# Attention over a long cache on one core: V of B in one megabyte transfer a step, issued by ScalarE instead of SyncE

## The chip, the cores and the metric

One core of a Trainium2 chip runs the whole program. The metric is device time in microseconds (us), as the median of several executions. Before: 859.62 us, median of 3 runs (857.61 to 861.04). With one core there is no second die to compare with.

## The reference, cut to what matters

Two attention blocks stand side by side, and their outputs are concatenated. A has 32 query heads on 4 K/V heads; B has 32 query heads on 32 K/V heads. B therefore reads eight times as much cache as A.

```python
B, Sq, D = 16, 32, 1024
Hq, Hkv, Sk, Dh = 32, 4, 1024, 128     # A;  B: H = 32 heads of K and V
q = (x @ wq) ...                        # per head
scores = einsum("bhqd,bhkd->bhqk", q, k) * Dh ** -0.5
p = softmax(scores)
o = einsum("bhqk,bhkd->bhqd", p, v)
out = o ... @ wo                        # bf16; A and B concatenated
```

K and V of B are 134 MB each, out of 338 MB that are read.

## The kernel before: the parts that matter

The kernel records operations with the buffers that they read and write. A list scheduler then puts them in order with a model of their durations, and each engine gets its own stream of instructions in that order. Semaphore waits are inserted. Each engine works through its own stream in order, and the streams meet only at semaphores.

There are 128 steps for B. A step needs 1 MB of K and 1 MB of V (four heads of one batch element); A's K and V, wq and wo come in between. K has two buffers and V has three. K goes through a DVE transpose, PE makes the scores, ScalarE the exponentials, PE transposes P, and then PE makes the product with V (L947, "the product" below). The product frees V's buffer.

```python
def st_dmaV(q):                                   # V of B; all loads are issued by "sp", SyncE
    ...
    sl = q.vslot                                  # t % 3
    for t_ in range(2):                           # two transfers of 512 KB
        vsrc = pb["v"][q.b, q.h0 + 2 * t_:q.h0 + 2 * t_ + 2].rearrange("a (p c) d -> p a c d", c=NCH)
        pr.add("sp", lambda e, ...: e.dma_start(VB_sb[:, sl, 2 * t_:2 * t_ + 2, :, :], vsrc),
               writes=[("VB", sl, t_)], dma_key=f"vb{sl}_{t_}", name="vb_dma", dur=2 * Sk * Dh * 2, ...)
```

The scheduler's model has one line for the DMA. It holds SyncE's loads back, so that none is issued more than 1.5 us before the modelled DMA is free. This hold applies to `"sp"` alone.

```python
if op.eng == "sp":
    st = max(st, dma_free[0] - SP_AHEAD)          # 1.5 us; SyncE's loads only
...
if op.dma_key is not None:
    free[op.eng] = st + 0.06                      # cost of an issue on its engine
    xs = max(st + 0.06, dma_free[0])              # first in, first out
    dma_free[0] = xs + op.dur / dma_bw
    op.t1 = dma_free[0] + dma_lat
...
seq = sorted(range(n), key=lambda k: (ops[order[k]].t0, k))   # the order of all streams
```

On the chip nothing holds SyncE back except the semaphores. The model gives the order alone.

## Time and profile before

| | before |
|---|---|
| time, median | 859.62 us |
| busy: PE, DVE, ACT | 84%, 63%, 52% |
| DMA, 40 to 835 us | 407 GB/s |
| DMA idle, worked out from the trace's packets | 15.6 us, of which 12.3 in the last 25 us and 1.2 in the middle |
| V of B: mean time from landing to its product | 1.9 us |

"DMA idle" is the busy time of the packets in each microsecond, summed over the 16 DMA engines and divided by 16, taken from one. I worked it out from the packet records. "Middle" is from 40 us to 25 us before the end.

These are lines of the page of before: busy time of the engines, busy tenths and GB/s in 40 slices, the one DMA queue, the chain that ended last by engine, two groups (line, engine, operation, tiles, count, then busy us and mean ns of one, then idle time just before them with what ended most of it), and DMA issues (KB each, median us to landing).

```profile
PE 717.3 (84%) x11970; PEld 436.2 (51%) x12098; DVE 541.5 (63%) x1115; ACT 447.1 (52%) x981; POOL 67.9 (8%) x76
...
DMA  9999999999999999999999999999999999999994
GB/s 341 366 400 412 413 412 389 413 415 399 413 400 385 413 410 412 402 400 411 403 412 404 406 411 401 411 408 408 413 403 412 412 409 412 414 411 409 411 384 174
...
q1 hardware_dynamic: 135424, 339.78, 101.1%
...
DMA 53%; PE 19%; DVE 15%; SPq 6%; issue 4%; ACT 2%; POOL 1%; POOLq 0%; DVEq 0%
...
L820 DVE STREAM_TRANSPOSE KBt_sb<-KB_sb 128x1024 f32<-128x1024 f32 x256 | 306.1, 1226 | 97.7 <-DMA KB_sb<-in_B_k_cache_dram 93.9
...
L947 PE MATMUL ps_o<-VB_sb,PT_sb 128*32 128x128 bf16 x4096 | 81.6, 221 | 23.7 <-DMA VB_sb<-in_B_v_cache_dram 16.6
...
KB_sb<-in_B_k_cache_dram SPq DMA_DIRECT2D x128, 1024.0 KB, 9.1
VB_sb<-in_B_v_cache_dram SPq DMA_DIRECT2D x256, 512.0 KB, 9.8
...
wq_sb<-in_A_wq_dram SPq DMA_DIRECT2D x32, 256.0 KB, 8.5
woB_sb<-in_B_wo_dram SPq DMA_DIRECT2D x32, 256.0 KB, 10.8
```

The DMA row of the slices is full to the last slice. The row of GB/s and the queue at 101.1% say the same: the DMA is the bound.

Windows of before (stretch; length; busy time of PE, PEld, DVE, ACT, POOL; granted clock; DMA share; GB/s), and the first projection in its timeline:

```profile
40.00:835.00 795.00, 679.54 (x11507) 415.32 (x11618) 515.91 (x1067) 430.40 (x948) 65.56 (x63) 0.97 1.03 407
```

```profile
17.01 3.47 PE L668 MATMUL ps_pj<-xT_sb,wq_sb 128*128 128x512 bf16 x8 [0.88 <-DVE xT_sb L584]
```

### The profile page before, as it was taken

What the parts mean: (1) busy time and instruction counts of PE and PEld (TensorE: products, weight loads), DVE (VectorE), ACT (ScalarE), POOL (GpSimd) and SP (SyncE); (2) the same over time, 40 slices, a digit from 0 to 9 for tenths busy, and PEclk for the clock granted to TensorE, in tenths of its full rate; (3) what the DMA queues carried; (4) which work ended last, traced back from release to release, by engine and by line L of the source; (5) the groups of instructions that cost most, each with busy time, mean ns of one, the idle gap of its engine ahead of it and who ended that gap; (6) DMA issues with size and microseconds to landing.
All of it is one profiled execution on the core that took longest, in us unless ns stands there. A gap on an engine that the chain in (4) does not pass through costs nothing.

```text
span 857.6 us, 27298 instructions
## 1 busy us (share of the span) xinstructions
PE 717.3 (84%) x11970; PEld 436.2 (51%) x12098; DVE 541.5 (63%) x1115; ACT 447.1 (52%) x981; POOL 67.9 (8%) x76
## 2 busy tenths in 40 slices
PE   3999998898978789888897979988889778878885
PEld 2546655455545455555554545545455445545452
DVE  1655566666657477577674756757777656666674
ACT  1456766466544464546554545544565554555452
POOL 0001000100000000000000000000000000000000
PEclk9999999999999999999999989999999999999898
DMA  9999999999999999999999999999999999999994
GB/s 341 366 400 412 413 412 389 413 415 399 413 400 385 413 410 412 402 400 411 403 412 404 406 411 401 411 408 408 413 403 412 412 409 412 414 411 409 411 384 174
DMA packets 135547, 341.57 MB, mean 398 GB/s; under 512 B 10496, under 2 KB 26880, under 8 KB 119040
## 3 DMA queue, kind: packets, MB, share of 16 engines
q1 hardware_dynamic: 135424, 339.78, 101.1%
q8 instruction: 96, 1.57, 0.7%
q14 instruction: 27, 0.22, 0.1%
HBM read 337.64 MB, written 2.10 MB: 396 GB/s over the span
## 4 chain that ended last, share of the span: by engine, by line
DMA 53%; PE 19%; DVE 15%; SPq 6%; issue 4%; ACT 2%; POOL 1%; POOLq 0%; DVEq 0%
DMA KB_sb<-in_B_k_cache_dram 40%; DVE KBt_sb L820 12%; DMA VA_sb<-in_A_v_cache_dram 5%; PE ps_pj L709 4%; PE ps_s L855 3%; DMA woA_sb<-in_A_wo_dram 3%; PE ps_pj L651 3%; PE ps_pj L668 2%; SPq L800 2%; PE ps_o L947 2%; PE ps_kt L913 2%; SPq L682 1%; PE ps_s L838 1%; PE ps_pt L897 1%; DMA woB_sb<-in_B_wo_dram 1%
## 5 line engine op out<-in xcount | busy, mean ns | idle before, releaser
L820 DVE STREAM_TRANSPOSE KBt_sb<-KB_sb 128x1024 f32<-128x1024 f32 x256 | 306.1, 1226 | 97.7 <-DMA KB_sb<-in_B_k_cache_dram 93.9
L878 ACT ACTIVATE P_sb<-ps_s 128x512 bf16<-128x512 f32 x256 | 152.4, 600 | 84.1 <-PE ps_s L855 74.5
L870 ACT ACTIVATE PTA_sb<-ps_s 128x1024 bf16<-128x1024 f32 x128 | 131.3, 1026 | 104.2 <-PE ps_s L838 91.5
L855 PE MATMUL ps_s<-KBt_sb,QB_sb 32*32 32x512 bf16 x4096 | 146.9, 395 | 10.1 <-DVE KBt_sb L820 5.5
L582 ACT COPY PT_sb<-ps_pt 128x512 f32<-128x512 f32 x128 | 74.9, 585 | 105.7 <-PE ps_o L947 88.6
L794 POOL COPY VAp_sb<-VA_sb 128x1024 bf16<-128x1024 bf16 x64 | 66.6, 1041 | 761.9 <-DMA VA_sb<-in_A_v_cache_dram 729.4
L897 PE MATMUL ps_pt<-id,P_sb 128*128 128x128 f32 x512 | 105.5, 305 | 9.3 <-ACT P_sb L878 7.3
L947 PE MATMUL ps_o<-VB_sb,PT_sb 128*32 128x128 bf16 x4096 | 81.6, 221 | 23.7 <-DMA VB_sb<-in_B_v_cache_dram 16.6
L897 PEld LDWEIGHTS ps_pt<-id,P_sb 128*128 128x128 f32 x512 | 82.7, 206 | 35.2 <-ACT P_sb L878 17.7
L947 PEld LDWEIGHTS ps_o<-VB_sb,PT_sb 128*32 128x32 bf16 x4096 | 60.0, 97 | 60.2 <-issue 56.9
L913 PE MATMUL ps_kt<-VAp_sb,PTA_sb 128*128 128x129 bf16 x1024 | 80.8, 222 | 10.9 <-POOL VAp_sb L794 4.9
L913 PEld LDWEIGHTS ps_kt<-VAp_sb,PTA_sb 128*128 128x128 bf16 x1024 | 67.5, 99 | 36.5 <-POOL VAp_sb L794 14.9
L838 PE MATMUL ps_s<-QT_sb,KTA_sb 128*128 128x256 bf16 x512 | 82.2, 275 | 3.0 <-DVE KTA_sb L584 2.0
L855 PEld LDWEIGHTS ps_s<-KBt_sb,QB_sb 32*32 32x32 bf16 x4096 | 49.3, 90 | 60.9 <-DVE KBt_sb L820 10.6
L709 PE MATMUL ps_pj<-woA_sb,OTA_sb 128*128 128x512 bf16 x224 | 64.0, 394 | 17.4 <-DMA woA_sb<-in_A_wo_dram 10.0
L963 DVE TENSOR_SCALAR OB_sb<-ps_o,rinv_all 128x128 bf16<-128x128 f32 x128 | 43.7, 342 | 53.4 <-PE ps_o L947 52.6
L709 PE MATMUL ps_pj<-woB_sb,OTB_sb 128*128 128x512 bf16 x206 | 62.0, 394 | 16.6 <-ACT OTB_sb L582 4.5
L668 PE MATMUL ps_pj<-xT_sb,wq_sb 128*128 128x512 bf16 x234 | 64.2, 389 | 8.4 <-DMA wq_sb<-in_B_wq_dram 3.4
L651 PE MATMUL ps_pj<-xT_sb,wq_sb 128*128 128x512 bf16 x232 | 63.9, 380 | 8.3 <-DMA wq_sb<-in_A_wq_dram 4.1
L883 DVE TENSOR_TENSOR stat<-stat 64x1 f32<-64x1 f32 x256 | 41.9, 164 | 32.0 <-ACT P_sb L878 24.4
L838 PEld LDWEIGHTS ps_s<-QT_sb,KTA_sb 128*128 128x128 bf16 x512 | 45.0, 98 | 25.5 <-issue 4.4
L722 DVE TENSOR_TENSOR acc<-acc,ps_pj 128x512 f32<-128x512 f32 x64 | 43.0, 672 | 20.1 <-PE ps_pj L709 19.7
(49 smaller groups left out, 533.0 us busy)
## 6 DMA issues: line engine op xcount, KB each, us to landing
KB_sb<-in_B_k_cache_dram SPq DMA_DIRECT2D x128, 1024.0 KB, 9.1
VB_sb<-in_B_v_cache_dram SPq DMA_DIRECT2D x256, 512.0 KB, 9.8
KA_sb<-in_A_k_cache_dram SPq DMA_DIRECT2D x64, 256.0 KB, 10.3
VA_sb<-in_A_v_cache_dram SPq DMA_DIRECT2D x64, 256.0 KB, 9.6
wq_sb<-in_B_wq_dram SPq DMA_DIRECT2D x32, 256.0 KB, 8.6
wq_sb<-in_A_wq_dram SPq DMA_DIRECT2D x32, 256.0 KB, 8.5
woB_sb<-in_B_wo_dram SPq DMA_DIRECT2D x32, 256.0 KB, 10.8
woA_sb<-in_A_wo_dram SPq DMA_DIRECT2D x32, 256.0 KB, 10.1
```

The source lines that it names most:

```text
L582: pr.add("act", lambda e: e.copy(dst_ap, src_ap), reads=reads, writes=writes, name=name + "@act", wtag=wtag, rtag=rtag)
L651: last = e.matmul(ps_pj[:, 0:tn], wq_sb[:, 0, j, hc * Dh:(hc + 1) * Dh], xT_sb[:, 0, j, t0:t0 + tn], start=(j == 0), stop=(j == DJ - 1))
L668: last = e.matmul(ps_pj[:, 0:NTOK], w, xT_sb[:, 1, j, :], start=(j == 0), stop=(j == DJ - 1))
L709: last = e.matmul(ps_pj[:, 0:OUTW], OT[:, gp, hh, :], wo_[:, hh, oh * OUTW:(oh + 1) * OUTW], start=(hh == 0), stop=(hh == nh - 1))
L820: pr.add("dve", lambda e: e.transpose(KBt_sb[:, sl, t_, :].bitcast(F32).rearrange("p (s r i) -> p s r i", r=2, i=32), KB_sb[:, rs, t_, :]. ...
L838: last = e.matmul(ps_s[:, sbf, c2, i * 2 * P:(i + 1) * 2 * P], KTA_sb[:, sl, c * P:(c + 1) * P], qt, start=True, stop=True)
L855: last = e.matmul(ps_s[32 * cg:32 * cg + 32, sbf, g, :].rearrange("p (sh cl j) -> p sh cl j", sh=4, cl=4), lhsT, kt[32 * a:32 * a + 32, g, ...
L870: pr.add("act", lambda e: e.activation(dst, src, ACTF.Exp, scale=scale), writes=BK_S[sbf] + [("PTA", q.half)], name="expA", rtag={("Sv", s ...
L878: pr.add("act", lambda e, src=src, dst=dst, g=g: e.activation(dst, src, ACTF.Exp, scale=scale, accum_out=st[:, g:g + 1]), writes=[BK_S[sbf ...
L897: last = e.transpose(ps_pt32[:, m * P:(m + 1) * P], p32[:, m:Sk // 2:NPK], id32[:])
L913: last = e.matmul(ps_kt[:, qh * OA0:qh * OA0 + Dh + 1], PTA_sb[:, h, c, qh * P:(qh + 1) * P], VAp_sb[:, sl, 4 * h + c, 0:Dh + 1], start=(h ...
L947: last = e.matmul(ps_o[32 * a:32 * a + 32, 0:Dh], PT_pairs[:, c // 2, 32 * (a ^ (c // 4 * 2)):32 * (a ^ (c // 4 * 2)) + 32, c % 2], VB_sb[ ...
```

## The change

The intent is to take 256 issues from SyncE and to let V be requested as soon as its buffer is free, by ScalarE, in transfers twice as large. (In the page of after, ScalarE's loads show as a DMA queue of their own, q10.) The scheduler also gets a more honest cost for an issue.

```diff
+DMA_ISSUE = 0.45
...
-                free[op.eng] = st + 0.06
-                xs = max(st + 0.06, dma_free[0])
+                free[op.eng] = st + DMA_ISSUE
+                xs = max(st + DMA_ISSUE, dma_free[0])
...
-                for t_ in range(2):
-                    vsrc = pb["v"][q.b, q.h0 + 2 * t_:q.h0 + 2 * t_ + 2].rearrange("a (p c) d -> p a c d", c=NCH)
-                    pr.add("sp", lambda e, t_=t_, vsrc=vsrc: e.dma_start(VB_sb[:, sl, 2 * t_:2 * t_ + 2, :, :], vsrc), writes=[("VB", sl, t_)],
-                           dma_key=f"vb{sl}_{t_}", name="vb_dma", dur=2 * Sk * Dh * 2, wtag={("VB", sl, t_): q.kid})
+                vsrc = pb["v"][q.b, q.h0:q.h0 + 4].rearrange("a (p c) d -> p a c d", c=NCH)
+                pr.add("act", lambda e: e.dma_start(VB_sb[:, sl, :, :, :], vsrc), writes=[("VB", sl)],
+                       dma_key=f"vb{sl}", name="vb_dma", dur=4 * Sk * Dh * 2, wtag={("VB", sl): q.kid})
...                                        (the product's reads follow: ("VB", kvs) in place of two halves)
```

V is now an `"act"` operation, so the scheduler no longer holds it back.

More of the change, by code (lines that the diff above doesn't have):

```diff
@@ L211, in odur @@
             if op.dma_key is not None:
-                return 0.06 + op.dur / dma_bw + dma_lat
+                return DMA_ISSUE + op.dur / dma_bw + dma_lat
             return op.dur
@@ L950, in st_pv @@
             for c0 in range(0, NCH, 2):
-                pr.add("pe", lambda e, c0=c0: e_pv(e, c0), reads=["PT", ("VB", kvs, 0), ("VB", kvs, 1)], writes=[BK_O], name="PVB",
-                       dur=0.116, tag="B%d" % q.t, rtag={"PT": q.qid, ("VB", kvs, 0): q.kid, ("VB", kvs, 1): q.kid}, wtag={"Ops": q.qid})
+                pr.add("pe", lambda e, c0=c0: e_pv(e, c0), reads=["PT", ("VB", kvs)], writes=[BK_O], name="PVB",
+                       dur=0.116, tag="B%d" % q.t, rtag={"PT": q.qid, ("VB", kvs): q.kid}, wtag={"Ops": q.qid})
         def st_recip(q):
```

## The prediction

> **What bounds the kernel now.** The DMA. In the slices of the page the 16 DMA engines are busy nine tenths or more in 39 of 40, and the queue table puts 101.1% of their span on one queue. Between 40 and 835 us they move 407 GB/s; the transposes of K (the costliest DVE group) wait 93.9 us for K to land, and the chain that ended last is 53% DMA, 40% of it loads of K of B. PE is busy 84%, DVE 63%, ACT 52%. From 20 us to the last steps at least 12 packets are in flight at nearly every moment. A fit of packet counts per 3 us stretch gives 80 ns of a DMA engine for a 2 KB packet (92160 of them, V among them), 313 ns for 8 KB (16384, K) and 44 ns for 1 KB (16384): together, with semaphore writes, about 839 us of 16 engines. The rest of 858 is the start (2 to 3 us) and a tail of some 15 us, where the last slice falls to 174 GB/s.
>
> **What the change does.** It removes no byte and leaves V's packets at 2 KB; only 128 transfers fewer complete: 2048 semaphore packets of 9 to 10 ns, 1.3 us over 16 engines. SyncE loses 256 issues (170 us of its sequencer in the trace, 0.47 us median, up to 3.2 us when some 1400 descriptors are outstanding). ScalarE gains 128 issues, each of 512 descriptors; my estimate from SyncE's 0.34 us (128 descriptors) and 0.47 us (256) is 0.5 to 0.9 us, so 65 to 115 us: ScalarE's occupancy rises from 52% to 60 to 65%. With 2% of the chain, this costs almost nothing. SyncE's waits no longer hold V back, but they never emptied the DMA engines, so there is little to gain. The Trainium skill ("DMA: Bandwidth & Descriptors", section "Issuing engines are not separate DMA queues") says that both issuers share the same 16 DMA engines and that a second one saves only sequencer time; this trace, with one issuer, cannot show it.
>
> **Where it can cost.** At the start the three V buffers are free, so ScalarE issues 3 MB of V at once, which competes with x, wq and the first K. The projections start at 17.0 us now; I expect 20 to 23 us. As V is then already loaded, the DMA engines have less to do while compute starts: 1 to 5 us lost. In the steady state V is always ahead and K shares bandwidth with it; buffers fill instead, and the DMA engines stay busy: zero change. In the tail the last K rather than the last V lands late: 0 to 3 us more.
>
> **Sum.** 859.6 - 1.3 + 3 (start) + 0 (steady) + 1 (tail) = about 862 us; range 850 to 877. Faster by over 2%: 0.07; within 2%: 0.80; slower: 0.13.
>
> **What would show each step.** A second DMA queue with about 134 MB; 40 to 835 us still at 400 to 415 GB/s; V issues on ScalarE's queue of 0.5 to 0.9 us and no waits there of many microseconds; first projection later than 17.0 us; K of B still the main DMA of the chain; PE's waits for V gone.
>
> **What would make it wrong.** If ScalarE blocks in a V issue (backpressure, or a wait for the product that frees V's buffer), the exponentials are late and PE, at 84%, becomes the bound: slower by 2 to 5%. If two rings let a DMA engine overlap packets better than one, the 80 ns per 2 KB packet falls and the kernel gains 1 to 3%. If K gets too small a share beside V, its transposes, scores and all buffers stall together: slower.

## More of the kernel before

Waits of before (engine, line, releaser: us in total, times, longest us):

```profile
DVE KBt_sb L820 <- DMA KB_sb<-in_B_k_cache_dram: 93.9, 82, 3.1
...
PE ps_o L947 <- DMA VB_sb<-in_B_v_cache_dram: 16.6, 27, 1.6
```

DVE waits often for K, but never long. PE waits little for V. Waits of PE and of its weight loads overlap, so I quote matmuls only.

All loads stand in SyncE's queue, and each needs about 9 us from issue to landing although 1 MB alone takes about 2.6 us at 407 GB/s. That is a backlog, and it keeps the DMA fed.

## The result, and the profile after

The changed kernel took 902.78 us (median of 4 runs, 896.74 to 909.97). Before, in the same rounds: 859.26 us (857.61 to 861.04). The ratio is 1.0509, with a 95% interval of 1.0425 to 1.0594: slower by 5%. Ratios here are the mean time of one kernel's fast runs over that of the other's of the same rounds, so not quite the ratio of the medians that are quoted.

The same lines of the page of after:

```profile
PE 731.2 (81%) x11975; PEld 442.2 (49%) x12098; DVE 539.2 (60%) x1115; ACT 447.0 (49%) x981; POOL 67.9 (8%) x76
...
DMA  9998999989999999999999999999899999999892
GB/s 347 411 360 296 369 409 405 410 321 415 379 402 414 414 357 392 390 412 406 405 402 406 411 392 400 410 406 356 303 408 363 401 369 414 411 403 409 284 383 83
...
q1 hardware_dynamic: 65792, 205.55, 57.6%
q10 hardware_dynamic: 67584, 134.23, 39.5%
...
DMA 46%; PE 31%; DVE 14%; ACT 3%; issue 2%; SPq 2%; POOL 1%; ACTq 0%; DVEq 0%; POOLq 0%
...
L820 DVE STREAM_TRANSPOSE KBt_sb<-KB_sb 128x1024 f32<-128x1024 f32 x256 | 306.1, 1224 | 60.6 <-DMA KB_sb<-in_B_k_cache_dram 52.0
...
L947 PE MATMUL ps_o<-VB_sb,PT_sb 128*32 128x128 bf16 x4096 | 84.8, 227 | 49.0 <-DMA VB_sb<-in_B_v_cache_dram 40.7
...
VB_sb<-in_B_v_cache_dram ACTq DMA_DIRECT2D x128, 1024.0 KB, 11.6
KB_sb<-in_B_k_cache_dram SPq DMA_DIRECT2D x128, 1024.0 KB, 8.2
...
wq_sb<-in_A_wq_dram SPq DMA_DIRECT2D x32, 256.0 KB, 10.9
woB_sb<-in_B_wo_dram SPq DMA_DIRECT2D x32, 256.0 KB, 12.6
```

Total bytes are the same, and there are two queues, 205.55 and 134.23 MB, as predicted. But the DMA row has gaps and the GB/s row has holes (296, 321, 303, 284). PE stands idle 49.0 us before the product with V, instead of 23.7, most of it for V's transfer. ScalarE's own busy time is unchanged.

```profile
DVE KBt_sb L820 <- DMA KB_sb<-in_B_k_cache_dram: 52.0, 45, 3.8
...
PE ps_o L947 <- DMA VB_sb<-in_B_v_cache_dram: 40.7, 21, 4.4
```

DVE waits less for K than before, and PE's matmuls wait 40.7 us for V instead of 16.6. So V, which was to be early, is late before 21 of the products. At the same time V is early elsewhere: from landing to its product it now waits 7.3 us on average, instead of 1.9.

Windows of after: the middle, and two neighbouring stretches of 4 us.

```profile
40.00:835.00 795.00, 656.88 (x10921) 398.96 (x11031) 485.27 (x1011) 409.48 (x904) 60.91 (x59) 0.94 1.00 389
181.00:185.00 4.00, 4.00 (x25) 2.67 (x23) 1.63 (x4) 1.61 (x2) 0.00 (x0) 0.57 1.00 411
185.00:189.00 4.00, 3.83 (x55) 2.41 (x55) 3.93 (x6) 2.87 (x6) 1.04 (x1) 1.00 0.47 128
```

In the second stretch the DMA moves 411 GB/s while PE runs at a granted clock of 0.57; in the third the DMA share drops to 0.47 and 128 GB/s. PE's timeline around it:

```profile
163.25 0.63 PE L947 MATMUL ps_o<-VB_sb,PT_sb 128*32 128x128 bf16 x32 [1.22 <-DMA VB_sb<-in_B_v_cache_dram]
...
180.61 0.60 PE L710 MATMUL ps_pj<-woB_sb,OTB_sb 128*128 128x512 bf16 x2 [1.27 <-DMA woB_sb<-in_B_wo_dram]
...
192.44 0.63 PE L947 MATMUL ps_o<-VB_sb,PT_sb 128*32 128x128 bf16 x32
```

No product ran between 163.9 and 192.4 us. PE was at projections and at A meanwhile, and it waited for one of the wo loads at 180.6 (that load had been issued at 164.06 and took 16.4 us). No product means that no V buffer comes free, and between 178.90 and 187.66 us neither engine issued a load. But a stretch without a product need not leave the DMA idle: in before, 19.2 us pass without one (51.4 to 70.6) while the DMA moves 405 GB/s. Nor does this hole need the second queue. It stands at the same place of the same order when SyncE issues V (e3 below): no product from 158.1 to 185.8 us, and within that

```profile
180.00:184.00 4.00, 3.83 (x33) 2.54 (x28) 3.91 (x8) 1.93 (x6) 1.04 (x1) 1.00 0.52 153
```

In both runs SyncE stood in this hole at a K issue until DVE had transposed the K before and so freed its buffer (8.6 us here, 6.1 in e3). So this hole comes with the new order and not with the second queue. Idle DMA is the loss, whatever caused it.

The accounts close. The DMA idle time rose from 15.6 to 48.9 us (33.3 more: 27 in the middle, 6 in the tail, none at the start). The packets took 883.4 us of 16 engines instead of 873.0, so 10.4 more. Together that is 43.7 of the 45.6 us by which the profiled spans differ (903.2 and 857.6). The granted clock of PE fell too, from 0.972 to 0.938. The Trainium skill ("TensorE: Matmul & The Clock Gate", "What's actually happening") says that the clock halves after an idle window of about 3.4 us; the trace agrees as far as its half-clock stretches last 3.4 us or multiples of it (the one that the end cuts off aside), and there are 20 of them instead of 12. It does not bear out that PE must be idle all that time: in the 3.4 us before each of the 20, PE was busy for 0.3 to 1.9 us. Whether the slower PE added to the loss or only followed from it was not tested. Why the packets took longer I don't know (two queues are not needed for it: in e5, with one queue, they took 907 us); their median by size is unchanged, and the mean of a 2 KB packet on V's queue is 86.8 ns, where it was 84.8 before.

The first projection, for the start:

```profile
16.51 3.58 PE L669 MATMUL ps_pj<-xT_sb,wq_sb 128*128 128x512 bf16 x8 [0.88 <-DVE xT_sb L585]
```

### The profile page after: what moved, and what is told of

Its sections match the earlier page's. It is cut to its first block, busy times and chain, and to the rows that moved or that the text cites. A ratio compares the mean times of both kernels' runs of the same rounds, so it can differ in the third digit from the quotient of the medians.

```text
span 903.2 us, 27179 instructions
## 1 busy us (share of the span) xinstructions
PE 731.2 (81%) x11975; PEld 442.2 (49%) x12098; DVE 539.2 (60%) x1115; ACT 447.0 (49%) x981; POOL 67.9 (8%) x76
## 3 DMA queue, kind: packets, MB, share of 16 engines
q1 hardware_dynamic: 65792, 205.55, 57.6%
q10 hardware_dynamic: 67584, 134.23, 39.5%
## 4 chain that ended last, share of the span: by engine, by line
DMA 46%; PE 31%; DVE 14%; ACT 3%; issue 2%; SPq 2%; POOL 1%; ACTq 0%; DVEq 0%; POOLq 0%
DMA VB_sb<-in_B_v_cache_dram 17%; DMA KB_sb<-in_B_k_cache_dram 16%; DVE KBt_sb L820 10%; DMA VA_sb<-in_A_v_cache_dram 7%; PE ps_pj L710 7%; PE ps_s L855 6%; PE ps_kt L913 3%; PE ps_pj L652 3%; PE ps_o L947 3%; PE ps_pt L897 2%; PE ps_s L838 2%; PE ps_pj L669 2%; DMA KA_sb<-in_A_k_cache_dram 2%; DMA woB_sb<-in_B_wo_dram 2%; PE ps_kt L811 2%
## 5 line engine op out<-in xcount | busy, mean ns | idle before, releaser
L855 PE MATMUL ps_s<-KBt_sb,QB_sb 32*32 32x512 bf16 x4096 | 149.3, 399 | 18.7 <-DVE KBt_sb L820 14.9
L947 PE MATMUL ps_o<-VB_sb,PT_sb 128*32 128x128 bf16 x4096 | 84.8, 227 | 49.0 <-DMA VB_sb<-in_B_v_cache_dram 40.7
L897 PE MATMUL ps_pt<-id,P_sb 128*128 128x128 f32 x512 | 106.4, 311 | 12.6 <-ACT P_sb L878 9.1
L947 PEld LDWEIGHTS ps_o<-VB_sb,PT_sb 128*32 128x32 bf16 x4096 | 61.7, 99 | 84.8 <-issue 39.2
L913 PE MATMUL ps_kt<-VAp_sb,PTA_sb 128*128 128x129 bf16 x1024 | 78.8, 224 | 8.3 <-POOL VAp_sb L795 5.5
L652 PE MATMUL ps_pj<-xT_sb,wq_sb 128*128 128x512 bf16 x231 | 68.6, 415 | 10.4 <-DMA wq_sb<-in_A_wq_dram 5.5
L669 PE MATMUL ps_pj<-xT_sb,wq_sb 128*128 128x512 bf16 x232 | 64.4, 399 | 8.5 <-ACT QT_sb L583 2.3
L710 PE MATMUL ps_pj<-woA_sb,OTA_sb 128*128 128x512 bf16 x229 | 60.5, 383 | 10.4 <-DMA woA_sb<-in_A_wo_dram 2.9
## 6 DMA issues: line engine op xcount, KB each, us to landing
VB_sb<-in_B_v_cache_dram ACTq DMA_DIRECT2D x128, 1024.0 KB, 11.6
wq_sb<-in_A_wq_dram SPq DMA_DIRECT2D x32, 256.0 KB, 10.9
woB_sb<-in_B_wo_dram SPq DMA_DIRECT2D x32, 256.0 KB, 12.6
```

What stands on the lines that cost most here:

```text
L652: last = e.matmul(ps_pj[:, 0:tn], wq_sb[:, 0, j, hc * Dh:(hc + 1) * Dh], xT_sb[:, 0, j, t0:t0 + tn], start=(j == 0), stop=(j == DJ - 1))
L669: last = e.matmul(ps_pj[:, 0:NTOK], w, xT_sb[:, 1, j, :], start=(j == 0), stop=(j == DJ - 1))
L710: last = e.matmul(ps_pj[:, 0:OUTW], OT[:, gp, hh, :], wo_[:, hh, oh * OUTW:(oh + 1) * OUTW], start=(hh == 0), stop=(hh == nh - 1))
L855: last = e.matmul(ps_s[32 * cg:32 * cg + 32, sbf, g, :].rearrange("p (sh cl j) -> p sh cl j", sh=4, cl=4), lhsT, kt[32 * a:32 * a + 32, g, ...
L897: last = e.transpose(ps_pt32[:, m * P:(m + 1) * P], p32[:, m:Sk // 2:NPK], id32[:])
L913: last = e.matmul(ps_kt[:, qh * OA0:qh * OA0 + Dh + 1], PTA_sb[:, h, c, qh * P:(qh + 1) * P], VAp_sb[:, sl, 4 * h + c, 0:Dh + 1], start=(h ...
```

## The experiments

Theories, as they stood before the first runs: S, the coarser transfer; I, the issue constant; O, the order that the scheduler made with V not held back; Q, the second queue. The later ones are named in the expectations. A patch after scheduling makes it possible to separate order from queue: the model sees V on one engine, and the emitted program issues it from another. The streams of PE, DVE, ACT (apart from the V issues), POOL and SyncE (apart from them too) were compared and are identical to the instruction in the pairs named below.

### Size and constant

e1: only the transfer is made whole, `"sp"` kept.

```diff
-                for t_ in range(2):  ... pr.add("sp", ... 512 KB)
+                pr.add("sp", lambda e: e.dma_start(VB_sb[:, sl, :, :, :], vsrc), writes=[("VB", sl)], ...)
```

> Only the size is changed: V of B as one transfer of 1 MB, still from SyncE, issue cost in the scheduler's model as before. Theory S (the coarser transfer makes the product wait and frees the buffer late): 875 to 905 us. Theories Q (second queue), O (order) and I (issue constant): within 1% of before, 855 to 866 us, at 395 to 400 GB/s over the span.

Measured: 861.51 us, ratio 1.0024 [0.9999, 1.0050]. Theory S falls.

e2: only `DMA_ISSUE = 0.45`.

> Only the constant is changed: the scheduler's model charges 0.45 us an issue, V in halves from SyncE. Theory I (the constant alone upsets the order): 875 us or more. Theories S, Q and O: 853 to 868 us; the order of the engines differs from before, but the schedule was made for one queue.

Measured: 858.37 us, ratio 0.9999 [0.9956, 1.0042]. Theory I falls. This order differs from before too (3638 lines in PE's stream; e1's by 4690), so a different order need not cost anything.

### Order against queue

e3: the changed kernel's schedule, V issued by SyncE. e4: e1's schedule, V issued by ScalarE.

```diff
             eng, emit, reads, writes, dma_key, name, dur, tag, prio = self.specs[order[k]]
+            if name == "vb_dma":
+                eng = "sp"       # e3: scheduled as "act";   e4: eng = "act", scheduled as "sp"
```

> The schedule is the changed kernel's to the instruction on PE, DVE, ACT and POOL; only V is issued by SyncE at the place where its time in the schedule puts it, so there is one queue again. Theory O (the schedule made with V unthrottled is what is slow): 885 us or more, DMA idle in the middle as in the changed kernel. Theory Q (two queues that share bandwidth break the order in which data is needed): 855 to 870 us, DMA never idle in the middle.

Measured: 883.36 us, ratio 1.0249 [1.0200, 1.0299] (by the 2% rule "unclear", but clearly above 1), so nearly half of the loss comes back. It lies between the two expectations. V landed in 8.8 us on average (11.6 in the changed kernel), and PE no longer waited for V. But SyncE's queue was blocked by V itself. Waits of SyncE in e3:

```profile
SPq L802 <- PE ps_o L949: 215.5, 70, 8.4
```

SyncE stood at a V issue until the product had freed the buffer, and K behind it was not asked for.

> The counterpart: the schedule is that of the one-transfer run to the instruction (V placed by the model as a SyncE load, held back with the other loads), but V is issued from ScalarE. Theory Q: 885 us or more. Theory O: 855 to 870 us. If both this and its counterpart lie in the middle, the two add.

Measured: 989.31 us, ratio 1.152 [1.1461, 1.1578]. Nothing but the issuer changed against e1, at the same places of the same order, and it cost 128 us. Q had the direction, but nobody expected the size. The trace says what it is. Waits of e4, and ScalarE's timeline in a stretch where the DMA was idle (the window below it: DMA share 0.23, 38 GB/s):

```profile
PE ps_o L949 <- DMA VB_sb<-in_B_v_cache_dram: 137.3, 55, 7.1
```

```profile
349.86 0.59 ACT L585 COPY PT_sb<-ps_pt 128x512 f32<-128x512 f32 x1 [2.12 <-PE ps_o L949]
350.65 0.27 ACT L585 COPY OTB_sb<-ps_o 128x128 bf16<-128x128 bf16 x1 [0.21 <-PE ps_o L970]
351.31 1.02 ACT L872 ACTIVATE PTA_sb<-ps_s 128x1024 bf16<-128x1024 f32 x1 [0.38 <-PE ps_s L840]
353.28 1.01 ACT L585 COPY KTA_sb<-ps_kt 128x1024 bf16<-128x1024 bf16 x1 [0.95 <-PE ps_kt L813]
354.19 0.27 ACT L585 COPY OTB_sb<-ps_o 128x128 bf16<-128x128 bf16 x1
354.78 0.60 ACT L880 ACTIVATE P_sb<-ps_s 128x512 bf16<-128x512 f32 x1 [0.32 <-PE ps_s L857]
354.79 0.37 ACTq L802 DMA_DIRECT2D VB_sb<-in_B_v_cache_dram  x1
```

```profile
350.00:354.00 4.00, 3.81 (x69) 2.25 (x76) 4.00 (x7) 2.45 (x4) 0.00 (x0) 1.00 0.23 38
```

The buffer for this V had been free since 343.31, when the product of three steps before ended. The issue left at 354.79. In between ScalarE was not at its limit, and no wait for the buffer held it: it worked through its stream, in which the copy of P waits for PE (349.86, released by a product that had itself waited for a V). SyncE, at the same place of the same order, runs ahead of all this. On average V was asked for 10.9 us after its buffer was free in e4 and 5.5 us in e1. Of 85 us of idle DMA in the middle of e4, 84 fall while a V buffer was free and not yet asked for. (This count, here and below, seems to take in about the first microsecond after an issue. Up to the start of the issue alone it is 83 in e4, 2.4 in the changed kernel, 1.2, 4.0 and 23.5 in e6, e9 and e10, 11.5 in e11, 25.7 in e13 and 104.4 in e14.)

### The place of the issue

e5 and e6 keep e1's order and move V's issue to where the model says that its buffer is free, on SyncE (e5) and on ScalarE (e6). e9 and e10 put it a quarter and six tenths of the way back to the held place, on ScalarE.

```diff
+        for op in ops:
+            if op.name == "vb_dma":
+                free_at = max([d.t1 + lat + DMA_MARGIN_DEFAULT for d in op.deps], default=0.0)
+                op.t0 = free_at + F * (op.t0 - free_at)    # F = 0 (e5, e6), 0.25 (e9), 0.6 (e10)
         seq = sorted(range(n), key=lambda k: (ops[order[k]].t0, k))
```

> The schedule of the one-transfer run (861.5 us) to the instruction on PE, DVE, ACT and POOL, V from SyncE, but each V issue is put into SyncE's stream where the model says its buffer is free, not where the model held it back. Theory E (V issued early on one queue delays K and the weights behind it; this is what made the run with the changed kernel's order 883 us): 875 to 895 us, with V landing well before its product. Rival P (what costs there is the order of PE and the others, which the early V entailed): 858 to 868 us.

Measured: 984.35 us, ratio 1.1441 [1.1403, 1.1479], far beyond the expectation. V landed 12.7 us (median) before its product, so it was not V that was late. SyncE was blocked by V's wait again:

```profile
SPq L803 <- PE ps_o L950: 235.6, 74, 11.0
```

> The same early places, but V is issued by ScalarE; all other orders are again those of the one-transfer run. The run with the late places on ScalarE took 989 us. Theory C (there the V issue stands in ScalarE's stream behind work that itself waits for the product of the V before, so that V is asked for 10.9 us after its buffer is free on average): early places remove most of it: 865 to 905 us, with the issue less than 3 us after the buffer is free. Rival B (two queues sharing bandwidth cost it): still 950 us or more.

Measured: 906.32 us, ratio 1.0549 [1.0520, 1.0579], 1 us above its expectation. V was asked for 0.4 us after its buffer was free, and 83 of e4's 128 us are back. So theory C, the lateness of an issue in ScalarE's stream, is what made most of e4. But 45 us remain, about as many as in the changed kernel. Waits of e6:

```profile
PE ps_pj L674 <- DMA wq_sb<-in_B_wq_dram: 27.2, 20, 2.4
...
PE ps_o L952 <- DMA VB_sb<-in_B_v_cache_dram: 14.6, 11, 2.6
```

Now it is wq that is late: it lands after 12 to 13 us on average (loads of the first 40 us left out), against 8.1 (A) and 9.5 (B) in e1. In this run the start lost time as well: the first projection began at 24.0 us (16.4 in e1), since 3 MB of V went first and PE waited 12.8 us for x of B. In the changed kernel 3 MB of V go first too, but its order loads x of B before wq, and the first projection was not late.

> V from ScalarE, all other orders those of the one-transfer run, and V's place in ScalarE's stream a quarter of the way from the early place (906 us) to the held-back one (989 us). Theory A (the early place costs because V takes bandwidth from what is needed sooner; a short hold-back trades that against lateness): 885 to 905 us, PE's waits for wq below the 24.7 us of the early place, V asked for 2 to 4 us after its buffer is free. Rival C (any delay in ScalarE's stream feeds back on itself): 915 us or more.

Measured: 904.78 us, ratio 1.0510 [1.0493, 1.0528], at the edge of theory A; V was asked for 2.5 us after its buffer was free.

> The same at six tenths of the way. Theory A: 900 to 940 us, V asked for 4 to 8 us after its buffer is free. Rival C: 945 us or more. In both, if no place of V in ScalarE's stream comes within 2% of before (877 us), the second queue costs time under this schedule wherever the issue stands.

Measured: 898.68 us, ratio 1.0429 [1.0405, 1.0453], 1 us below theory A's range; V was asked for 6.3 us after its buffer was free. Waits of e10:

```profile
PE ps_o L953 <- DMA VB_sb<-in_B_v_cache_dram: 58.0, 35, 4.3
...
PE ps_pj L675 <- DMA wq_sb<-in_B_wq_dram: 7.2, 9, 1.4
```

The waits move from wq to V, and the sum hardly changes. Idle DMA in the middle is 22, 24 and 29 us for F = 0, 0.25 and 0.6; the part of it in which a V buffer was free and not asked for rises from 4 to 12 to 25 us. There is a flat stretch near 900 us, and then at F = 1 the 989 us of e4. None of the places tried on ScalarE comes within 4% of before.

### Shares between the queues

In the changed kernel's trace, where both queues had transfers under way and SyncE's side was K with 8 KB packets, K moved at 300 GB/s and V, with 2 KB packets, at 111. (Counted again over other stretches: 296 and 123.) Beside SyncE's 1 KB packets (wq) it was 129 for wq and 258 for V; here the recount gives 106 and 296. So the queue with the larger packets gets more bytes, though not in full proportion: 300 GB/s of 8 KB packets against 111 of 2 KB are 1.5 packets of V for each of K, not one. e8 makes K's packets 2 KB; e7 is the control on one queue.

```diff
-  e.dma_start(KB_sb[:, sl, :, :].rearrange("p i n -> p (i n)"), ksrc)
+  [e.dma_start(KB_sb[...][:, 1024 * j:1024 * j + 1024], ksrc[:, 1024 * j:1024 * j + 1024]) for j in range(4)]
```

> A control: before, with each K of B loaded by four transfers of 256 KB whose packets are 2 KB instead of 8 KB. From the fit of packet times (4 times 80 ns against 313 ns) I estimate 7 us more: 862 to 872 us.

Measured: 876.57 us, ratio 1.0212 [1.0178, 1.0247] (again "unclear" by the 2% rule, but clearly above 1). My estimate of 7 us was too small; it is 17.

> The changed kernel with the same small K packets. In its trace, where both queues had work, [...]K with 8 KB packets moved at 300 GB/s and V with 2 KB packets at 111. Theory H (V lands late because it gets a packet's share, not half of the bytes): beside small K packets V moves at 180 to 220 GB/s, V's mean time to landing falls from 11.6 us to 9 to 10.5, K's rises above 9.5, PE's waits for V (68 us) fall below half. The whole time can go either way, as K is then late: 880 to 915 us. Rival C (V is late because of ScalarE's stream): V's time to landing stays above 11 us and PE's waits for V stay.

Measured: 911.80 us, ratio 1.0624 [1.0585, 1.0663]. All of theory H's figures hold (its 68 us are the waits of PE's matmuls and weight loads together, 40.7 and 27.4): V moves at 186 GB/s beside K's 208, lands in 10.1 us instead of 11.6, K (all four parts) needs 10.0 us, and PE waits less for V:

```profile
PE ps_o L948 <- DMA VB_sb<-in_B_v_cache_dram: 15.3, 9, 3.7
```

Yet the time does not follow. Against its control the changed kernel loses 35 us, where it lost 44 with large packets. So the share of bytes made V late, and taking that away left most of the loss.

e11 tries the same with e10's place of the issue.

> The six-tenths place on ScalarE (899 us) with K of B in 2 KB packets, whose control on one queue took 876.6 us. Theory H in its strong form (the second queue costs because V gets a small share of bytes beside K's 8 KB packets): within 2% of that control, below 894 us. Rival C (what is left is the tie of the V issue to ScalarE's stream, and the order of arrival, whatever the shares): 895 to 920 us, with most of the idle DMA time still while a V buffer is free and not asked for.

Measured: 926.97 us, ratio 1.0798 [1.0762, 1.0834], 50 us over the control. The strong form of theory H falls; the time is above the rival's range too. Of 19 us of idle DMA in the middle, 14.5 fall while a V buffer was free and not asked for.

### Another tensor on ScalarE

e12: V on SyncE as in e1, the weights on ScalarE at their places.

```diff
+            if name in ("wq_dma", "woA_dma", "woB_dma"):
+                eng = "act"
```

> V stays on SyncE in one transfer, all orders are those of the one-transfer run (861.5 us), and only the weights wq and wo (33.5 MB of 338) are issued from ScalarE at the same places. Theory D (the harm grows with what the second queue carries and how closely compute follows it): 858 to 880 us, PE waiting more for wq and wo. Rival (any second queue that runs beside SyncE's upsets the order of arrival as V does): 890 us or more. If it is 850 us or less, the second queue used this way is a gain.

Measured: 950.96 us, ratio 1.1092 [1.1036, 1.1148]. Theory D is wrong: a tenth of the bytes costs 89 us. Waits of e12:

```profile
PE ps_pj L671 <- DMA wq_sb<-in_B_wq_dram: 43.8, 22, 4.3
...
PE ps_pj L712 <- DMA woA_sb<-in_A_wo_dram: 27.9, 9, 5.6
```

The median time from issue to landing did not rise (wq of A 7.6 us, wo of B 3.5 us; 8.5 and 10.8 in before), so these loads are late because they were asked for late. It is the same tie as in e4, with a tensor that hardly competes for bandwidth.

### The changed kernel's own order, with V held back

The share of the order was open: e3 had SyncE blocked.

```diff
+        # used_at[op]: the model's start of the product that reads this V
+        for op in ops:
+            if op.name == "vb_dma":
+                op.t0 = max(op.t0, used_at[op] - L)     # L = 8 (e13 on SyncE, e14 on ScalarE), 12 (e15 on ScalarE)
```

> The changed kernel's order to the instruction on PE, DVE, ACT and POOL; V from SyncE, placed 8 us (of the scheduler's model, about the median that the one-transfer run has) before its product, so V waits no longer block SyncE. If the order is harmless and the issue is what costs: 855 to 870 us. If the order itself costs: 875 us or more.

Measured: 902.65 us, ratio 1.0511 [1.0486, 1.0536]. With V on SyncE this order is slow wherever V was put: 883 early, 903 held. This is not yet the order's cost alone, for 26.7 of the 27 us of idle DMA in the middle fall while a V buffer was free and not asked for; V stood behind K's waits in SyncE's stream. My 8 us may be a bad place for that order.

> The changed kernel with the same held-back places, but from ScalarE. From the 989 us of the counterpart with the other order, theory C (an issue in ScalarE's stream is late when placed late): 930 to 1000 us, the idle DMA time nearly all while a V buffer is free and not yet asked for. Rival (V running ahead was the whole cost in the changed kernel): 855 to 885 us.

Measured: 1019.37 us, ratio 1.1897 [1.1828, 1.1965]. One of the four runs (1027.54 us) was slow and is in both figures; the median of the three fast ones is 1015.52. The reading does not hang on it. Of the profiled run (fast), 105.0 of 105.5 us of idle DMA in the middle fall while a V buffer was free and not asked for. Theory C's direction, above its range.

> The same with 12 us ahead, so that only the longest leads (the model of the changed kernel has 7 to 36 us, median 14) are cut. Theory A plus C (too early delays others, too late is late): 890 to 915 us, no better than the changed kernel's 903 by more than 1.5%. Rival (running ahead is the whole cost): below 885 us.

Measured: 938.87 us, ratio 1.0958 [1.0904, 1.1012], slower than theory A plus C had it. The rival, that running ahead is the whole cost, falls with both.

All together, in us (the first order is e1's, made for V on a held-back SyncE queue; the second is the changed kernel's):

| order | SyncE, held | SyncE, early | ScalarE, early | ScalarE, between | ScalarE, held |
|---|---|---|---|---|---|
| e1's | 861.5 | 984.4 | 906.3 | 904.8, 898.7 | 989.3 |
| the changed kernel's | 902.7 (8 us) | 883.4 | 902.8 (the change) | 938.9 (12 us) | 1019.4 (8 us) |

No version beats before. e2, at 858.4 us, is the same.

## Why the prediction was wrong, point by point

- Right: the DMA bounds the kernel, the bytes and the packet sizes stay, the second queue carries 134 MB, ScalarE is not at its limit. Its issues take 0.37 us, less than my 0.5 to 0.9, and it was hardly blocked at them: in the changed kernel it stood idle before its 128 V issues for 17 us in all.
- The step that failed: "In the steady state V is always ahead and K shares bandwidth with it; buffers fill instead, and the DMA engines stay busy: zero change." V was not always ahead (PE waited for it 21 times, 40.7 us in all), and the buffers that filled did not keep the DMA busy: its idle time in the middle grew by 27 us, and 40 to 835 us ran at 389 GB/s instead of 407.
- What was behind it: I took the busy DMA engines for a property of the kernel, when they came from one queue in an order made for it. What the runs show: the same transfers at the same places of the same order, issued from ScalarE, cost 128 us (e1, e4), most of it because the issue then comes when ScalarE's stream gets there, and that stream follows PE. SyncE's runs further ahead (V asked for 5.5 us after its buffer was free, against 10.9). Placing the issue early cures this lateness and gives back 83 us (e6), but 37 to 45 us stay at each place tried up to six tenths (e6, e9, e10). The changed kernel places the issue early too (0.7 us after the buffer was free), so lateness is not what cost it its 44 us. Whether these have the same cause as e6's 45 is not shown, as its order is another.
- What is argued, not shown, is the cause of those last 44 us. The trace points to the order of arrival: V lands 7.3 us before its product on average, while wo of B takes 12.6 us (10.8 before) and wq of A 10.9 (8.5), PE's fixed stream waits for whichever is late, and the buffers that fill meanwhile leave the DMA idle (in only 7.5 of the 29 us a V buffer was free and not asked for). The new order itself is a rival that stays open: e3 has it on one queue, and there the DMA is still idle for 13 us in the middle (1.2 in before), part of it in the same hole at 180 us. But no experiment took the order of arrival away alone. Equal shares for V and K (e8) gave back 8 us against the control. Putting V back on SyncE with the changed order gave back 19.4 (e3) or nothing (e13). Order and issue interact, so the 44 us cannot be split into parts that add.
- Start: I expected the first projection at 20 to 23 us and 1 to 5 us lost. It began at 16.5 us, and idle DMA in the first 40 us was 2.1 us in both. The new order loads x of B first; e6, without that, began its first projection 7.6 us later than e1.
- "PE's waits for V gone" was wrong the other way: 40.7 us, from 16.6. "K of B still the main DMA of the chain" was wrong: V had 17% of it and K 16%.
- Among the things that could make it wrong I had named a blocked ScalarE and a small share for K. The trace shows neither: ScalarE was free, and it was V whose share was small.

## What to carry to other kernels

A load that is issued from a compute engine is asked for when that engine's in-order stream reaches it; before moving loads there from an engine that only issues, ask how far ahead of compute the old issuer ran and who must finish before the new one gets to it (here: 5.5 us after the buffer was free from SyncE, 10.9 from ScalarE, at the same place of the order). Full DMA engines in a profile are the joint work of one queue's order and the engines' order, so a change to who issues, or to what the scheduler holds back, must be tested with the order kept fixed. When two queues run together, compare their packet sizes: the one with the larger packets got more bytes here (300 GB/s against 111).

## What the Trainium skill lacked or had wrong

- "DMA: Bandwidth & Descriptors", section "Issuing engines are not separate DMA queues": it says that initiating on several engines only saves sequencer time. The runs agree that no bandwidth is gained (the fullest of 40 slices moved 415 GB/s before and after), but the page lacks that moving an issue can cost: 861.5 to 989.3 us with all orders kept (e1, e4), 951.0 us with a tenth of the bytes (e12).
- The same page, section "Queues, rings and completion order": it says that a DMA engine goes round robin between rows by packets. With records of 2 KB on both queues the shares are nearly equal, as that would have it (208 GB/s against 186, e8). What the page lacks is the consequence for two unequal streams: 300 GB/s against 111 with records of 8 and 2 KB, which is 1.5 records of V to one of K.
- The same page, section "Rules for kernel authors": for the highest bandwidth it asks for at least 1 MiB per DMA. Here two transfers of 512 KB and one of 1 MB gave the same (ratio 1.0024, e1), in a kernel whose DMA was idle for 1.2 us of the middle. K in 2 KB packets cost 17 us (e7; there each transfer was also cut into four of 256 KB, and the two were not separated).
- I found nothing on that page about an issue that blocks its engine while much is outstanding: an issue took 0.33 to 0.37 us at least, but up to 5.0 us for 256 KB on SyncE with some 1800 to 2000 descriptors outstanding in the changed kernel. V's issues on ScalarE, of 512 descriptors each, never took over 0.53 us there.
